# Agent attention and a maxout layer on one core: paired key tiles, 256-column output products, and the rare path's transfers on another queue

## The chip, the cores and the metric

The kernel runs on one core of one Trainium2 chip. The metric is the device time of one execution in microseconds (us). The kernel before took 259.56 us, the median of three runs (258.92 to 260.03).

## The reference

Four batches of 12,544 queries, keys and values of width 128, and 49 agents per batch. Agents attend over all keys, each query then attends over the 49 agents, and a layer with the maximum of three linear maps follows.

```python
def sm(a, b):
    s = scale * (a @ b.transpose(0, 2, 1))
    e = np.exp(s - s.max(-1, keepdims=True))
    return e / (e.sum(-1, keepdims=True) + 1e-09)
agent_v = sm(agents, k) @ v          # 49 x 128 per batch
x = sm(q, agents) @ agent_v          # 12544 x 128 per batch
h = np.maximum(np.maximum(x @ w1, x @ w2), x @ w3)   # 768 wide
out = h @ w_out
```

Everything comes in and goes out in float32: 77 MB of q, k and v in, 25.7 MB out.

## The kernel before, in words

All work is cut into tiles of 128 rows. A chunk of keys is 7 tiles (KT), a group of queries 8 tiles (GT); there are 14 chunks per batch and 49 groups in all (48 of one batch each, numbers 0 to 47, and number 48 of what is left of all four). SP issues every load and store of the ordinary path: three query groups, or up to four chunks of keys or values, in one transfer, into one of five buffers LD; results leave from five buffers OS, three groups at a time (line 521). A buffer is loaded again when its last reader is done.

Keys and values of batch b, per chunk: POOL casts K to bfloat16 (kc, line 300), PE turns the tiles (kt, 305), DVE takes them out of PSUM (ke, 311), PE makes the scores of 128 keys by 49 agents (ks), ACT the exponentials (kx, 320), ACT or POOL casts V (vc), and PE adds up the value products (kv, values, 322). This is done in eight products: one with a matrix of ones as the stationary operand and all 343 exponentials as the moving one, for the totals, and per tile one with V as the stationary and 49 exponentials as the moving operand. All of a batch's chunks are added up in one PSUM bank, acc. When a batch is through, normalise (nr, 368) reduces the seven totals, takes the reciprocal and scales.

From a batch's 49 by 128 result follow the small steps that make its matrix G (128 rows): the hidden units are sorted into those that are decided for all agents, whose part of the layer is linear, and at most 64 open ones, which the query groups compute. G holds U and V columns for the open units (GU, GV), a linear part (GL, written by linear_out, 494) and output rows for open units (GW). Rows 0 to 63 and 64 to 127 hold the same for the two halves of a pair of query tiles: in EQ, the exponentials of a group, rows 0 to 48 belong to one tile of a pair and rows 64 to 112 to the other.

Queries, per group s: POOL casts (qc), PE turns (qt), ACT takes out (qe, 541), PE makes scores (sc), ACT exponentials (ex, 554), PE sums (su) and DVE reciprocals (re); PE makes u and v, ACT a rectifier (a, 574), DVE the maximum into R (x, 577); out_products (p, 579) makes the output in two PSUM banks: for EQ with GL and for R with GW, for each of four pairs and each half, one product of half the rows and 128 columns, 16 in all. DVE scales both banks into OS (ov, out_scale, 595), and SP stores.

The order of all this is a list written out by hand (ORDER) with the buffer of each result behind the stroke; each engine takes its steps in that order, and waits by semaphores are put in from the buffers that a step reads and writes.

At the end DVE checks that all totals are in range (c0, c1, worst) and writes one number, most. All five engines load it and branch (lines 262 and 263): if it is over 64, a general path of the whole computation is run, of some 17,600 instructions, 520 of them SP's; otherwise they jump over it. With these inputs they jump. Behind the jump SP waits for all transfers, and the program ends.

## Time and profile before

| | before |
|---|---|
| median of three runs | 259.56 us |
| the profiled execution | 258.95 us |
| its span, first to last instruction | 257.1 us |
| mean granted TensorE clock | 0.911 |
| PE, DVE, ACT, POOL busy | 73%, 65%, 56%, 57% |
| moved by the DMA engines | 105.01 MB, 409 GB/s over the span |
| HBM read and written | 78.74 MB, 25.69 MB |

In the profile, PE is TensorE's matmuls and PEld its weight loads, which overlap; DVE is VectorE, ACT ScalarE, POOL GpSimd, SP SyncE with its queue of transfers (SPq). The queue q1 holds SP's loads and stores, q10 ScalarE's one transfer (the agents, line 214), q8 and q14 the blocks of instructions that the engines fetch as they go. A row of a group names line, engine, operation, what is written and read, the count, then busy us and mean ns of one, then idle time before it with what ended it. A row of the timeline begins with its start and its busy time in us. Matmuls are pipelined, so the busy time of a row is longer than the distance from its start to the next row's.

### The profile page before, as it was taken

Reading aid. Unit: us, or ns where it says so; the run is one execution under the profiler, and the core shown is the slowest. Engines: PE = TensorE matmul, PEld = TensorE weight load, DVE = VectorE, ACT = ScalarE, POOL = GpSimd, SP = SyncE. Lnnn points to the kernel's source line nnn. Section 1 sums busy time; section 2 is a strip of 40 time slices with the busy share of each in tenths; the row PEclk is TensorE's granted clock in tenths of the full one; section 3 lists DMA queues with packets and bytes.
Section 4 is the critical chain, followed back from the end, with each engine's and each line's share of the span. In section 5 each row is a group of like instructions: output and inputs, shape, how many; then the busy total and the mean of one; then the engine's idle time right before and its main releaser. Section 6 shows DMA issues by size and latency. Waiting matters only on the chain.

```text
span 257.1 us, 7504 instructions
## 1 busy us (share of the span) xinstructions
PE 187.8 (73%) x3071; PEld 138.0 (54%) x3106; DVE 166.3 (65%) x344; ACT 145.2 (56%) x240; POOL 145.6 (57%) x164
## 2 busy tenths in 40 slices
PE   0684675779798679895988699868688789997500
PEld 0462543658476458674775486446465466664200
DVE  4444422837677878864599955744729989888830
ACT  1445356328585656573666657646256868796400
POOL 2252652988789289786973997478464434440000
PEclk9998699779999979997699999999869999999855
DMA  7999999999999999999999999999999999999992
GB/s 257 435 415 416 427 420 426 420 426 419 420 418 425 423 422 427 424 418 423 418 426 424 419 425 425 426 416 421 424 432 421 421 410 431 423 423 426 410 370 85
DMA packets 11528, 105.01 MB, mean 409 GB/s; under 512 B 1176, under 2 KB 2396, under 8 KB 4444
## 3 DMA queue, kind: packets, MB, share of 16 engines
q1 hardware_dynamic: 11280, 104.34, 97.0%
q8 instruction: 26, 0.43, 0.7%
q10 hardware_dynamic: 203, 0.10, 0.1%
q14 instruction: 19, 0.15, 0.1%
HBM read 78.74 MB, written 25.69 MB: 406 GB/s over the span
## 4 chain that ended last, share of the span: by engine, by line
DMA 55%; POOL 12%; PE 12%; DVE 8%; ACT 5%; issue 3%; another core or an unknown queue 1%; SPq 0%; DVEq 0%; ACTq 0%; POOLq 0%
DMA LD<-in_v_dram 25%; DMA LD<-in_k_dram 14%; DMA out_dram<-OS 9%; PE psum L273 9%; POOL VB L300 6%; DMA LD<-in_moe_w_dram 5%; DVE OS L595 3%; POOL KB L300 3%; POOL QB L535 3%; PE psum L305 3%; DMA sums_of<-in_agents_dram 2%; ACT EQ L554 1%; ACT VB L298 1%; ACT QT L541 1%; DVE R L577 1%
## 5 line engine op out<-in xcount | busy, mean ns | idle before, releaser
L300 POOL CAST KB<-LD 128x896 bf16<-128x896 f32 x56 | 51.8, 964 | 36.2 <-DMA LD<-in_k_dram 35.2
L535 POOL CAST QB<-LD 128x1024 bf16<-128x1024 f32 x49 | 49.7, 1048 | 34.7 <-DMA LD<-in_q_dram 26.0
L595 DVE TENSOR_TENSOR OS<-psum,sums_of 128x512 f32<-128x512 f32 x97 | 60.7, 676 | 9.7 <-DMA out_dram<-OS 5.0
L541 ACT ACTIVATE QT<-psum 128x1024 bf16<-128x1024 bf16 x49 | 50.2, 1024 | 21.9 <-PE psum L305 20.2
L311 DVE COPY KT<-psum 128x896 bf16<-128x896 bf16 x56 | 34.5, 620 | 34.0 <-PE psum L305 29.8
L305 PE MATMUL psum<-ident,KB 128*128 128x128 bf16 x392 | 37.8, 249 | 11.3 <-POOL KB L300 10.2
L300 POOL CAST VB<-LD 128x896 bf16<-128x896 f32 x42 | 38.5, 956 | 5.8 <-DMA LD<-in_v_dram 5.4
L554 ACT ACTIVATE EQ<-psum 128x512 bf16<-128x512 f32 x49 | 29.3, 598 | 21.9 <-PE psum L273 15.9
L320 ACT ACTIVATE EK<-psum 128x343 bf16<-128x343 f32 x56 | 25.3, 459 | 25.4 <-PE psum L273 16.6
L305 PEld LDWEIGHTS <-KB 128*128 128x128 bf16 x392 | 29.2, 113 | 17.9 <-POOL KB L300 14.0
L305 PE MATMUL psum<-ident,QB 128*128 128x128 bf16 x392 | 31.9, 228 | 6.5 <-POOL QB L535 5.8
L574 ACT ACTIVATE AS<-psum 128x512 bf16<-128x512 f32 x49 | 29.1, 597 | 12.8 <-PE psum L273 12.3
L577 DVE TENSOR_TENSOR R<-psum,AS 128x512 bf16<-128x512 f32 x49 | 32.4, 676 | 5.8 <-ACT AS L574 2.2
L305 PEld LDWEIGHTS <-QB 128*128 128x128 bf16 x392 | 26.1, 102 | 15.2 <-POOL QB L535 8.4
L273 PEld LDWEIGHTS <-EQ 49*128 49x128 bf16 (+1 forms) x588 | 20.8, 97 | 16.9 <-ACT EQ L554 8.0
L273 PE MATMUL psum<-QT,agT 128*128 128x512 bf16 (+1 forms) x82 | 25.2, 374 | 6.2 <-ACT QT L541 5.7
L273 PE MATMUL psum<-EQ,G 128*128 128x512 bf16 (+1 forms) x91 | 28.0, 367 | 1.3 <-issue 0.6
L273 PEld LDWEIGHTS <-VB 128*128 128x128 bf16 x392 | 16.8, 97 | 17.7 <-ACT VB L298 8.9
L273 PE MATMUL psum<-EK,VB 128*128 128x49 bf16 x392 | 19.6, 187 | 6.4 <-ACT VB L298 5.2
L273 PE MATMUL psum<-agT,KT 128*128 128x49 bf16 x392 | 20.7, 192 | 1.5 <-DVE KT L311 0.9
L273 PE MATMUL psum<-G,EQ 49*128 49x128 bf16 x392 | 20.9, 223 | 1.2 <-DVE OS L595 0.5
L273 PE MATMUL psum<-G,R 64*128 64x128 bf16 x392 | 20.1, 223 | 1.4 <-DVE R L577 1.4
(89 smaller groups left out, 184.7 us busy)
## 6 DMA issues: line engine op xcount, KB each, us to landing
LD<-in_q_dram SPq DMA_DIRECT2D x16, 1536.0 KB, 17.7
out_dram<-OS SPq DMA_DIRECT2D x15, 1536.0 KB, 22.1
LD<-in_k_dram SPq DMA_DIRECT2D x12, 1792.0 KB, 16.3
LD<-in_v_dram SPq DMA_DIRECT2D x12, 1792.0 KB, 17.0
LD<-in_k_dram SPq DMA_DIRECT2D x4, 896.0 KB, 16.7
LD<-in_v_dram SPq DMA_DIRECT2D x4, 896.0 KB, 15.0
out_dram<-OS SPq DMA_DIRECT2D x3, 512.0 KB, 12.3
LD<-in_moe_w_dram SPq DMA_DIRECT2D x3, 384.0 KB, 13.6
```

Source lines behind the costliest of these rows:

```text
L273: self.nc.tensor.matmul(out, w, x, start=start, stop=True, skip_group_check=True)
L298: self.nc.scalar.activation(out, src, AF.Copy)
L300: self.nc.gpsimd.tensor_copy(out=out, in_=src)
L305: self.nc.tensor.transpose(t[:, j * P:(j + 1) * P], src[:, j, :], self.ident)
L311: return lambda: self.nc.vector.tensor_copy(out=self.t[f"kT{r}"], in_=self.t[f"kT_ps{r}"].bitcast(BF16)[:, :KT * C])
L320: return lambda: self.nc.scalar.activation(self.t[f"e{r}"], self.t[f"s{r}"][:, :KT * A], AF.Exp, scale=SCALE)
L535: return lambda: self.nc.gpsimd.tensor_copy(out=self.t[f"qb.{s}"], in_=self.half("q", s))
L541: return lambda: self.nc.scalar.activation(self.t[f"qT.{s}"].rearrange("p j c -> p (j c)"), self.t[f"qT_ps.{s}"].bitcast(BF16), AF.Copy)
L554: return lambda: self.nc.scalar.activation(self.t[f"e.{s}"], self.t[f"qs.{s}"], AF.Exp, scale=SCALE)
L574: return lambda: self.nc.scalar.activation(self.t[f"a.{s}"], self.t[f"u.{s}"], AF.Relu)
L577: return lambda: self.nc.vector.tensor_tensor(out=self.t[f"r.{s}"], in0=self.t[f"v.{s}"], in1=self.t[f"a.{s}"], op=ALU.max)
L595: self.nc.vector.tensor_tensor(out=out, in0=src, in1=rc.unsqueeze(2).to_broadcast([P, 4, C]), op=ALU.mult)
```

## The change

Value products (values): the exponentials of a tile now lie 64 apart (EK is 7 x 64 wide, cleared once at the start), and V's buffers have two more columns per tile, filled with ones once. Two tiles' exponentials, 128 columns, are the stationary operand and two tiles of V with their ones, 260 columns, the moving one; tile by tile the two blocks on the diagonal are what is wanted. A chunk is three such products and one of a single tile (64 by 130), and the totals come with the ones columns. At a batch's end DVE copies the two blocks into one tile (ne), PE turns and adds them with two float32 products against a folded identity (nt), and normalise (nr) takes the reciprocal and scales.

Output products (out_products): G's parts GL and GW are twice as wide and block-diagonal, the upper half of the rows with one tile's columns, the lower with the other's. One product takes all 128 rows and makes 256 columns, both tiles of a pair: 8 instead of 16 per group. The outputs of a bank are now four tiles in a row, and the scores read every second tile. Linear_out becomes two copies.

The products with rd and with pick are put one after the other, three small tiles share memory with cand, and the loads and stores of the general path are issued by ScalarE instead of SP.

PE at the output products of group 36, ahead of which stands u of group 39; EQ_90 holds group 36's exponentials, G_138 (before) and G_149 (after) are batch 3's G. Before:

```order
L273 LDWEIGHTS G_138
L273 MATMUL psum<-EQ_93,G_138 128x512
L273 LDWEIGHTS EQ_90
L273 MATMUL psum<-G_138,EQ_90 128x128
L273 LDWEIGHTS EQ_90
L273 MATMUL psum<-G_138,EQ_90 128x128
L273 LDWEIGHTS EQ_90
L273 MATMUL psum<-G_138,EQ_90 128x128
L273 LDWEIGHTS EQ_90
L273 MATMUL psum<-G_138,EQ_90 128x128
```

The same place after, up to the first product with R:

```order
L285 LDWEIGHTS G_149
L285 MATMUL psum<-EQ_93,G_149 128x512
L285 LDWEIGHTS EQ_90
L285 MATMUL psum<-G_149,EQ_90 128x256
L285 LDWEIGHTS EQ_90
L285 MATMUL psum<-G_149,EQ_90 128x256
L285 LDWEIGHTS EQ_90
L285 MATMUL psum<-G_149,EQ_90 128x256
L285 LDWEIGHTS EQ_90
L285 MATMUL psum<-G_149,EQ_90 128x256
L285 LDWEIGHTS R_101
L285 MATMUL psum<-G_149,R_101 128x256
```

Nothing is moved past another step; eight products of 128 columns have become four of 256, for EQ and again for R.

PE in one chunk of keys, between the scores of one chunk and of the next; EK_96 holds exponentials, VB_78 the cast V. Before, the first rows of eight products:

```order
L273 MATMUL psum<-agT,KT_81 128x49
L273 LDWEIGHTS ones
L273 MATMUL psum<-EK_96,ones 128x343
L273 LDWEIGHTS VB_78
L273 MATMUL psum<-EK_96,VB_78 128x49
L273 LDWEIGHTS VB_78
L273 MATMUL psum<-EK_96,VB_78 128x49
```

After, all of them:

```order
L285 MATMUL psum<-agT,KT_81 128x49
L285 LDWEIGHTS EK_96
L285 MATMUL psum<-VB_78,EK_96 128x260
L285 LDWEIGHTS EK_96
L285 MATMUL psum<-VB_78,EK_96 128x260
L285 LDWEIGHTS EK_96
L285 MATMUL psum<-VB_78,EK_96 128x260
L285 LDWEIGHTS EK_96
L285 MATMUL psum<-VB_78,EK_96 64x130
L285 LDWEIGHTS KT_82
```

The product with ones, which read only exponentials, is gone, and the first product of a chunk now reads the cast V.

SP after its last stores; LD_65 is a load buffer. Before, the general path's loads follow the branch:

```order
L521 DMA out_dram<-OS_105 128x1024 x2
L521 DMA out_dram<-OS_105 128x512 x2
L262 TENSOR_LOAD most
L263 COMPARE_AND_BRANCH
L618 DMA LD_65<-in_k_dram 128x896 x15
L634 DMA LD_66<-in_v_dram 128x896
```

After, to the end of SP's program:

```order
L550 DMA out_dram<-OS_105 128x1024 x2
L550 DMA out_dram<-OS_105 128x512 x2
L274 TENSOR_LOAD most
L275 COMPARE_AND_BRANCH
L275 UNCONDITIONAL_BRANCH x2
```

SP's 520 instructions of the general path are one now, and ScalarE has 516 more in it (1428 instead of 912). In the ordinary part PE has 1224 instructions fewer, counting those that only wait (4990 instead of 6214).

The diff, cut to its core (ORDER has `ne` and `nt` put ahead of each `nr`, and nothing else):

```diff
-GU, GV, GL, GW, GC = 0, P, 2 * P, 3 * P, 4 * P
+GU, GV, GL, GW, GC = 0, P, 2 * P, 4 * P, 6 * P
+VC = C + 2
...
-            add(f"kv{r}", PE, em.values(b, g), mm(2 * KT, 49), after=[f"kx{r}", f"vc{r}"] + ([f"kv{b}.{g - 1}"] if g else []),
+            add(f"kv{r}", PE, em.values(b, g), mm(KT // 2, 2 * VC), after=[f"kx{r}", f"vc{r}"] + ([f"kv{b}.{g - 1}"] if g else []),
...
-        add(f"nr{b}", DVE, em.normalise(b), (0.62, 0.75), after=[f"kv{b}.{NCH - 1}"], use=[f"acc{b}"])
+        add(f"ne{b}", DVE, em.key_evacuate(b), (0.35, 0.5), after=[f"kv{b}.{NCH - 1}"], use=[f"acc{b}"])
+        add(f"nt{b}", PE, em.key_turn(b), (0.6, 0.85), after=[f"ne{b}"], use=[f"acc{b}"])
+        add(f"nr{b}", DVE, em.normalise(b), (0.25, 0.4), after=[f"nt{b}"], use=[f"acc{b}"])
...
+        self.fold = const.tile([P, A], FP32, name="fold")
+        for h in range(2):
+            nc.vector.tensor_copy(out=self.fold[h * H:(h + 1) * H, :], in_=self.ident[h * H:(h + 1) * H, h * H:h * H + A])
+        for e in self.slots["EK"]:
+            nc.vector.memset(e, 0.0)
+        for v in self.slots["VB"]:
+            nc.vector.memset(v[:, :, C:], 1.0)
...
     def values(self, b, g):
         def fn():
             acc, e, vb = self.t[f"acc{b}"], self.t[f"e{b}.{g}"], self.t[f"vb{b}.{g}"]
-            self.mul(acc[:, :KT * A], self.ones, e, g == 0)
-            for j in range(KT):
-                self.mul(acc[:, KT * H:KT * H + A], vb[:, j, :], e[:, j * A:(j + 1) * A], False)
+            for j in range(0, KT, 2):
+                n = min(2, KT - j)
+                self.mul(acc[:n * H, :n * VC], e[:, j * H:(j + n) * H], vb[:, j:j + n, :].rearrange("p j c -> p (j c)"), g == 0 and j == 0)
...
+    def key_evacuate(self, b):
+        def fn():
+            for h in range(2):
+                r = slice(h * H, (h + 1) * H)
+                self.nc.vector.tensor_copy(out=self.av[r, :], in_=self.t[f"acc{b}"][r, h * VC:(h + 1) * VC])
+    def key_turn(self, b):
+        def fn():
+            t = self.t[f"acc{b}"][:, 2 * VC:]
+            self.mul(t[:, :A], self.av[:, :C], self.fold, True)
+            self.mul(t[:, H:H + A], self.av[:, C:C + 1].to_broadcast([P, P]), self.fold, False)
...
-            self.nc.vector.tensor_reduce(out=kr, in_=acc[:, :KT * A].rearrange("p (j a) -> p a j", a=A), op=ALU.add, axis=AX)
-            self.nc.vector.reciprocal(kr, kr)
-            self.nc.vector.tensor_tensor(out=self.avT[b][:, :A], in0=acc[:, KT * H:KT * H + A], in1=kr, op=ALU.mult)
+            self.nc.vector.reciprocal(kr, t[:, H:H + A])
+            self.nc.vector.tensor_tensor(out=self.avT[b][:, :A], in0=t[:, :A], in1=kr, op=ALU.mult)
...
-            for src, c, k in (("e", GL, A), ("r", GW, H)):
+            for src, c in (("e", GL), ("r", GW)):
                 for jj in range(GT // 2):
-                    for h in range(2):
-                        r = slice(h * H, h * H + k)
-                        self.mul(self.t[f"o.{s}.{h}"][:, jj * C:(jj + 1) * C], self.t[f"{src}.{s}"][r, jj * P:(jj + 1) * P],
-                                 self.G[of[jj]][r, c:c + C], src == "e" and jj == 0)
+                    self.mul(self.t[f"o.{s}.{jj // 2}"][:, jj % 2 * 2 * C:(jj % 2 + 1) * 2 * C], self.t[f"{src}.{s}"][:, jj * P:(jj + 1) * P],
+                             self.G[of[jj]][:, c:c + 2 * C], src == "e" and jj % 2 == 0)
...
-            nc.sync.dma_start(kf[:, :KT, :], rows("k", b, g))
+            nc.scalar.dma_start(kf[:, :KT, :], rows("k", b, g))
...
-                nc.sync.dma_start(vf[:, :KT, :], rows("v", b, g))
+                nc.scalar.dma_start(vf[:, :KT, :], rows("v", b, g))
```

More of the change, by code (lines that the diff above doesn't have):

```diff
@@ L177, in graph @@
         add(f"x.{s}", DVE, em.max_second(s), dve(512), after=[f"v.{s}", f"a.{s}"], new=[("R", f"r.{s}")], use=[f"v.{s}", f"a.{s}"])
-        add(f"p.{s}", PE, em.out_products(s), (0.5, 0.72), after=[f"x.{s}", f"ex.{s}"] + gy, new=[("M", f"o.{s}.{h}") for h in range(2)],
+        add(f"p.{s}", PE, em.out_products(s), (0.9, 1.1), after=[f"x.{s}", f"ex.{s}"] + gy, new=[("M", f"o.{s}.{h}") for h in range(2)],
             use=[f"e.{s}", f"r.{s}"])
@@ L519, in fn @@
             if h is not None:
[L520 removed]
+                far, near = (x[:, 4 * h:4 * h + 4, :] for x in (far, near))
             self.nc.sync.dma_start(far, near)
         return fn
[L524 to L526 removed]
     def rc(self, s):
```

71 lines of the change are left out of this document (40 added, 31 removed).

## The prediction

> **What bounds the kernel now.** I read the page's slices and queues first, then busy time by stretch, then the end.
>
> ```profile
> PE 187.8 (73%) x3071; PEld 138.0 (54%) x3106; DVE 166.3 (65%) x344; ACT 145.2 (56%) x240; POOL 145.6 (57%) x164
> ...
> DMA  7999999999999999999999999999999999999992
> GB/s 257 435 415 416 427 420 426 420 426 419 420 418 425 423 422 427 424 418 423 418 426 424 419 425 425 426 416 421 424 432 421 421 410 431 423 423 426 410 370 85
> ...
> q1 hardware_dynamic: 11280, 104.34, 97.0%
> q8 instruction: 26, 0.43, 0.7%
> q14 instruction: 19, 0.15, 0.1%
> ...
> LD<-in_q_dram SPq DMA_DIRECT2D x16, 1536.0 KB, 17.7
> out_dram<-OS SPq DMA_DIRECT2D x15, 1536.0 KB, 22.1
> ```
>
> The DMA engines are full from the second slice to the last but two, at about 420 GB/s, and 97.0% of their time belongs to q1, the loads and stores. A transfer of 1.57 MB needs 3.7 us at that rate, yet lands 17.7 to 22.1 us after its issue: some 14 us of others stand ahead of it. The bytes do not change, so an engine that is late by less than that changes nothing until the last stores. The end has to be read by itself; here are the stretches from 199 us, when no load is left to issue, with busy us of PE, PEld, DVE, ACT, POOL, the clock, the DMA share and GB/s.
>
> ```profile
> 199.00:208.00 9.00, 6.66 (x84) 4.00 (x81) 8.47 (x21) 6.93 (x12) 4.10 (x5) 1.00 1.01 419
> 208.00:216.00 8.00, 7.80 (x148) 5.50 (x147) 7.21 (x16) 6.82 (x13) 4.00 (x4) 1.00 1.02 418
> 216.00:224.00 8.00, 7.53 (x129) 5.25 (x132) 6.92 (x16) 6.70 (x11) 3.01 (x3) 1.00 1.01 428
> 224.00:232.00 8.00, 7.38 (x119) 4.90 (x116) 6.75 (x14) 6.84 (x11) 3.01 (x3) 1.00 1.00 423
> 232.00:240.00 8.00, 6.57 (x101) 4.11 (x102) 7.02 (x16) 4.82 (x8) 0.00 (x0) 1.00 1.00 420
> ...
> 247.00:257.10 10.10, 0.00 (x0) 0.00 (x0) 0.00 (x0) 0.00 (x0) 0.00 (x0) 0.50 0.44 172
> ```
>
> Here PE and DVE are nearly full while the DMA still never idles; compute is finished at 247, and the DMA engines empty for ten microseconds more. The next lines are the chain's last piece; SP's queue of its last stores and its waits at the branch (line 263), from 240 us on; the DMA share of the last 27 us in 40 slices of 0.68 us, with the code blocks of that time and the landing of the last pair of stores.
>
> ```profile
> 246.67 0.16 DVE most L458
> ```
> ```profile
> 240.33 4.15 SPq L521 DMA_DIRECT2D out_dram<-OS  x4
> ```
> ```profile
> SPq L263 <- SPq L263: 7.7, 2, 6.8
> ```
> ```profile
> DMA  9999999999999999999999999877767531200000
> ...
> q8 instruction: 3, 0.05, 0.7%
> q14 instruction: 9, 0.07, 0.7%
> ...
> out_dram<-OS SPq DMA_DIRECT2D x2, 256.0 KB, 11.3
> ```
>
> The last store is issued at about 244 and lands 11.3 us later, at 255.3; the span ends 1.8 us after that. The verdict is known at 246.83; SP then waits at the branch twice, 7.7 us in all, which brings it from about 247.5 to that landing. From slice 26 (247 us) the share falls: some DMA engines are done, others go on to slice 35 (254 us). So the slowest DMA engine sets the end, and two paths run beside each other in the last ten microseconds: stores to land, and all engines taking the branch over the general path, for which code is fetched (9 of the 19 blocks of q14 fall in these 27 us).
>
> **Part 1, output products (out_products).** One group before is eight G,EQ and eight G,R products; rows of PE, start and busy us:
>
> ```profile
> 102.39 0.40 PE L273 MATMUL psum<-G,EQ 49*128 49x128 bf16 x8
> 102.63 0.39 PE L273 MATMUL psum<-G,R 64*128 64x128 bf16 x8
> 102.85 0.39 PE L273 MATMUL psum<-G,EQ 49*128 49x128 bf16 x8
> 103.08 0.39 PE L273 MATMUL psum<-G,R 64*128 64x128 bf16 x8
> 103.40 0.62 PE L305 MATMUL psum<-ident,QB 128*128 128x128 bf16 x8
> ```
>
> Two groups take 103.40 - 102.39 = 1.01 us, 0.50 each: 0.23 per eight, 29 ns per product of 128 columns, and 0.09 lost where it goes over to full-height products. The last row's products have 128 columns as well, at full height, and last 0.62 for eight, so the half-height ones overlap in pairs. After, eight full-height products of 256 columns. Their pace from 512 columns:
>
> ```profile
> 97.58 0.38 PE L273 MATMUL psum<-EQ,G 128*128 128x512 bf16 x1
> 97.80 0.38 PE L273 MATMUL psum<-QT,agT 128*128 128x512 bf16 x1
> ```
>
> 0.22 per 512, so 0.11 per 256 and 0.88 per group: +0.38 us, or +0.3 if the way into the half-height products costs as much as the way out. The Trainium skill, TensorEngine Tiling (Array Packing), Theoretical Speedup and Key Properties, gives up to twice the speed for at most 64 rows and a drain at each change of mode, which speaks against giving the tiles up: by it the group would grow by 0.46 and win the drains back, +0.37 for the one seen. The trace agrees, by 29 ns against 55 per 128 columns and by the 0.09. How many groups stand where:
>
> ```profile
> 0.00:199.40 199.40, 13.25 (x256) 9.17 (x256) 22.09 (x33) 0.92 1.00 417
> ```
>
> That is PE's time on the tile R: 256 products, 32 groups, before 199.4, so 17 of 49 after. The 32 cost 12 us of PE spread over 199, behind the queue of 14 us: nothing. For the last 17, PE gains 6.5 us of work. From 208 to 232 it has 24 - 22.71 = 1.3 us idle, and the 11 groups there add 4.2: 2.9 us late. From 232 to 240 it has 1.4 us idle against five groups' 1.9, but DVE sets the pace there. So the last store is issued D = 3 us later, at 247; bounds 0 (DVE hides it, since a first bank is complete two products earlier) and 6.5.
>
> **Does D move the end?** Not by the stores: the slowest DMA engine has work until about 254 and its share of the last stores comes before that as long as D is under some 8 us; the quick ones idle meanwhile. By the branch it may: 246.83 + D = 250 is left with 7 us to the end instead of 10.3. If those 10.3 are rigid, all 3 us show. If code is fetched at leisure beside the stores, none does. SP's two waits end with the landing, so SP had slack; of the other four engines no row tells. I take 0 for the likeliest, since after 250 the fetches meet engines at a share of 0.3 to 0.5 instead of 0.7.
>
> **Part 2, value products (values), k_exps, casts.** Rows of two groups before:
>
> ```profile
> 101.64 0.32 PE L273 MATMUL psum<-EK,ones 128*128 128x343 bf16 x1
> 101.79 0.34 PE L273 MATMUL psum<-EK,VB 128*128 128x49 bf16 x7
> 101.98 0.31 PE L273 MATMUL psum<-EK,ones 128*128 128x343 bf16 x1
> ```
>
> 0.34 per group; after, three of 260 columns and one of 130 at the pace above, 0.39. So 56 x 0.05 = 2.8 us more of PE, all before 199: 0. Added wait: the product with ones needed only the exponentials, now the first product waits for the cast of V too; behind it on PE stand transposes and scores of the next chunks, and POOL waits for their buffers. 0.15 us at a time, under the queue. If that cover were gone, it would be 56 x 0.2 = 11 us.
>
> **Part 3, totals.** Rows of what goes and of the nearest to what comes:
>
> ```profile
> L371 DVE TENSOR_REDUCE sums_of<-psum 128x49 f32<-128x343 f32 x4 | 2.0, 510 | 5.2 <-PE psum L273 5.2
> ...
> L494 DVE CAST G<-psum 128x256 bf16<-128x256 f32 x4 | 1.7, 425 | 4.2 <-PE psum L273 4.1
> ...
> L226 DVE MEMSET G<- 128x256 uint32 x4 | 1.1, 272 | 0.0
> ...
> L277 DVE CAST ag_bf<-sums_of 49x512 bf16<-49x512 f32 x1 | 0.9, 947 | 2.6 <-DMA sums_of<-in_agents_dram 2.6
> ...
> L284 DVE COPY slot_of<-psum 128x64 f32<-128x64 f32 x1 | 0.2, 217 | 0.0
> ```
>
> The reduction of 0.51 goes; two copies of 0.25 to 0.3 and two float32 products come, which the trace does not show: 0.2 us each as any small one, to 0.9 at four passes. Chain per batch: +0.4 to +1.9 us, four times. PE's new wait for the copies has behind it the next batch's first transposes in batch 0, for which DVE waits, and query products in the others, 0.6 us at a time. The order puts a batch's first query groups several microseconds behind it, and for batches 0 to 2 the DMA queue hides it. Batch 3 lies near 200 us: up to 1 us there, taken into D's bounds. Linear_out in two copies, +0.2 us on DVE per batch, likewise. The prologue gains four clears of EK (224 words, 0.24), G half as long again (4 x 0.14), four short fills and two casts: about 1.9 us on DVE, which idles 2.6 before ag_bf: 0. Tiles that now share cand's memory are used one after another as before, and the scores read as many columns of QT, every second tile: 0.
>
> **Part 4, fewer instructions.** PE loses 392 + 224 products with their weight loads and gains 8 pairs: 1216 instructions of 2 x 3106. The 26 q8 blocks are 0.43 MB / 26 = 16 KB each; taken as PE's stream, 239 instructions to a block, 5 go. One costs 0.7% x 16 x 257.1 / 26 = 1.1 us of one DMA engine; five are 5.5 us, spread over 16 engines 0.34. Bounds: 0 (blocks on engines that finish early) and -1.1 (one fewer on the slowest). I take -0.3. The Trainium skill, Runtime: NRT & Kernel Launch, Instruction fetch mechanics, gives blocks of 256 instructions and calls their cost mostly hidden, which would make this term 0; the 16 KB agree with it, the full DMA engines speak against hidden.
>
> **Part 5, the general path's transfers on ScalarE's queue.** They do not run. SP's code behind the branch becomes short, so perhaps two blocks of q14 fewer in the last 8 us: 0.7% x 16 x 27 / 9 = 0.34 us each on one engine. Between 0 and -0.7, and only if it is the slowest; 0. ACT, off the path there, jumps further.
>
> **Sum.** The profiled execution took 258.95: span 257.1 and 1.85 around it. -0.3 makes 258.65. The median of the runs shown is 0.61 higher, so 259.3.
>
> **Rivals.** A: DMA still sets the end, 259.3; its own range is 258.5 (blocks at -1.1 instead of -0.3) to 260.1 (no gain, 259.6, and the 0.5 us by which the runs shown lie above their median). For it: the full share to 247 and the emptying after; 0.70.
> B, slower: the verdict path. PE is late by D at 199 to 240 us, the branch follows, and code fetch ends after the last landing. It decides once D exceeds the slack of that path. With D = 3 and no slack 259.3 + 3 = 262.3; with half of it 260.8. For it: 7.80 of 8 busy on PE, 9 blocks fetched in the tail. Against: SP's waits. 0.20. The same page's section says that a taken branch outside the fetched window stalls for a fetch; that is this mechanism, and the late q14 blocks agree.
> C, faster: the slowest DMA engine loses a whole PE block and both of SP's: -1.1 - 0.7, so 257.8. For it: the taper from 247.7 to 254, in which single blocks weigh fully. Against: which engine serves them is not shown. 0.10. That the change does nothing to the time at all lies in A.
>
> A measurement of this kernel tells 0.5%, 1.3 us, from no change. C lies below 258.3, B's larger half above 260.9; the range 258.1 to 261.6 holds A whole, half of B and part of C. Faster 0.10, same 0.72, slower 0.18.
>
> **What would show it.** Right: bytes and share unchanged to 247 us; a group of output products at 0.85 to 0.9 us; 21 blocks on q8; the last store issued near 247 and landed by 255.3; span 256 to 258. B: the most row near 250 and SP's wait at the branch short, with idle DMA engines before the end. Wrong: the DMA share under 9 tenths before 240 us, PE above 95% there, or an end that moves by over 2 us with the last landing.

## The result and the profile after

| | before | after |
|---|---|---|
| median | 259.03 us (258.73 to 260.03, 18 runs) | 255.18 us (254.59 to 258.82, 18 runs) |
| after / before | | 0.9852, 95% interval 0.9838 to 0.9866 |
| the profiled execution | 258.95 us | 256.11 us |
| its span | 257.1 us | 254.3 us |
| mean granted TensorE clock | 0.911 | 0.948 |

The kernel became faster by 1.5%, 3.85 us; the forecast was no change, 259.3, with a range from 258.1. About 0.5 us of that distance is its base: it stood on a median of 259.56 us over three runs, and over 18 the kernel before takes 259.03. Below, a difference of two kernels in us is the difference of their ratios to the kernel before, times 259.0. Two of the runs of the kernel after, at 258.5 and 258.8 us, were disturbed and are left out of the ratio. The profiled execution of the kernel after, 256.11 us, lies 0.9 us above its median, so its span shows 2.8 of the 3.85 us.

The page of the kernel after: busy time, DMA share and GB/s in 40 slices of the span, and the queues.

```profile
PE 207.8 (82%) x2484; PEld 152.4 (60%) x2506; DVE 169.9 (67%) x362; ACT 146.2 (57%) x240; POOL 145.1 (57%) x164
...
DMA  6999999999999999999999999999999999999992
GB/s 251 439 430 418 432 426 426 432 422 435 422 418 426 428 430 427 428 427 422 431 424 434 423 432 426 428 426 424 426 425 429 425 421 430 422 427 425 399 401 80
...
q1 hardware_dynamic: 11280, 104.34, 97.2%
q8 instruction: 20, 0.33, 0.5%
...
q14 instruction: 16, 0.13, 0.1%
```

The queue q1 has the same 11280 packets and 104.34 MB as before, and the DMA engines are as full as before from the second slice on. But what they move in that time is more: most slices read 422 to 435 where most read 415 to 427. Busy time by stretch says it in one row. First the kernel before from 10 to 236 us (the last two numbers are the DMA share and GB/s), then the kernel after, with stretches that answer to those of the prediction:

```profile
10.00:236.00 226.00, 180.81 (x2983) 133.44 (x3017) 151.62 (x298) 138.59 (x229) 142.52 (x154) 0.93 1.01 422
```
```profile
10.00:236.00 226.00, 198.61 (x2408) 146.00 (x2428) 152.34 (x303) 138.35 (x228) 142.00 (x154) 0.95 1.01 427
...
208.00:216.00 8.00, 7.92 (x121) 6.27 (x122) 7.14 (x16) 6.16 (x12) 3.42 (x4) 1.00 1.01 428
...
232.00:240.00 8.00, 7.08 (x72) 5.08 (x71) 6.70 (x15) 6.23 (x9) 0.00 (x0) 1.00 0.98 407
...
247.00:254.30 7.30, 0.16 (x1) 0.00 (x0) 1.06 (x6) 0.00 (x0) 0.00 (x0) 0.59 0.29 112
```

At an equal share, 104.34 MB take 247.3 us at 422 GB/s and 244.4 us at 427: 2.9 us less, about what the span lost. Behind 247 us some 0.8 MB are left to move (112 GB/s over 7.3 us) instead of 1.7 (172 GB/s over 10.1 us), so the stores are done sooner. The transfers also land sooner (KB each, median us from issue to landing), the last pair of stores within 5.7 us:

```profile
LD<-in_q_dram SPq DMA_DIRECT2D x16, 1536.0 KB, 15.6
out_dram<-OS SPq DMA_DIRECT2D x15, 1536.0 KB, 18.3
...
out_dram<-OS SPq DMA_DIRECT2D x2, 256.0 KB, 5.7
```

TensorE's rows answer to the costs of the products; each begins with start and busy us:

```profile
64.95 0.67 PE L285 MATMUL psum<-VB,EK 128*128 128x260 bf16 x4
65.56 0.61 PE L285 MATMUL psum<-QT,agT 128*128 128x512 bf16 x2
...
239.90 0.60 PE L285 MATMUL psum<-G,EQ 128*128 128x256 bf16 x4
...
240.34 0.60 PE L285 MATMUL psum<-G,R 128*128 128x256 bf16 x4
...
240.77 0.24 PE L285 MATMUL psum<-sel,EQ 128*128 128x2 bf16 x4
...
242.15 3.97 SPq L550 DMA_DIRECT2D out_dram<-OS  x4
...
248.29 0.16 DVE L485 SCALAR_TENSOR_TENSOR most<-good,gap 128x1 int32<-128x1 f32 x1
```

A group of output products takes 240.77 - 239.90 = 0.87 us, as worked out; a chunk of value products takes 0.61 us, not 0.39. The verdict, and with it the last store's issue, comes 1.6 us later than before (248.29 against 246.67). SP's waits from 236 us on show that the end has changed hands (engine and line, waited for, us in total, times, longest):

```profile
SPq L275 <- SPq L275: 2.5, 2, 1.8
SPq L274 <- DVE most L485: 2.3, 1, 2.3
...
SPq L860 <- PEq L275: 1.0, 1, 1.0
```

At the branch SP waits 2.5 us instead of 7.7, and then, with all stores landed, 1.0 us for TensorE, which is still on its way over the general path (it branched at 249.1 and goes on at 253.3).

### The profile page after: what moved, and what is told of

Read it like the earlier page. It is cut to its first block, busy times and chain, and to the rows that moved or that the text cites. A ratio compares the mean times of both kernels' runs of the same rounds, so it can differ in the third digit from the quotient of the medians.

```text
span 254.3 us, 6336 instructions
## 1 busy us (share of the span) xinstructions
PE 207.8 (82%) x2484; PEld 152.4 (60%) x2506; DVE 169.9 (67%) x362; ACT 146.2 (57%) x240; POOL 145.1 (57%) x164
## 3 DMA queue, kind: packets, MB, share of 16 engines
q1 hardware_dynamic: 11280, 104.34, 97.2%
## 4 chain that ended last, share of the span: by engine, by line
PE 63%; DVE 12%; ACT 9%; DMA 7%; issue 4%; POOL 2%; ACTq 0%; DVEq 0%; POOLq 0%
PE psum L285 48%; PE psum L317 15%; DMA LD<-in_k_dram 5%; ACT QT L566 4%; DVE OS L618 3%; DMA sums_of<-in_agents_dram 2%; ACT EQ L579 2%; ACT VB L310 1%; DVE gap L435 1%; POOL KB L312 1%; ACT AS L599 1%; DVE KT L323 1%; DVE R L602 1%; DVE cand L434 1%; ACT EK L334 1%
## 5 line engine op out<-in xcount | busy, mean ns | idle before, releaser
L285 PE MATMUL psum<-VB,EK 128*128 128x260 bf16 x224 | 39.7, 279 | 4.9 <-ACT VB L310 3.0
L317 PE MATMUL psum<-ident,KB 128*128 128x128 bf16 x392 | 34.7, 238 | 4.2 <-POOL KB L312 3.4
L285 PEld LDWEIGHTS <-EK 128*128 128x128 bf16 x224 | 21.0, 102 | 24.4 <-issue 16.4
L285 PE MATMUL psum<-QT,agT 128*128 128x512 bf16 (+1 forms) x104 | 29.6, 371 | 6.1 <-ACT QT L566 5.9
L285 PEld LDWEIGHTS <-EQ 128*128 128x128 bf16 x392 | 25.7, 97 | 11.9 <-ACT EQ L579 6.9
L317 PEld LDWEIGHTS <-KB 128*128 128x128 bf16 x392 | 27.6, 107 | 8.5 <-POOL KB L312 4.0
L317 PE MATMUL psum<-ident,QB 128*128 128x128 bf16 x392 | 30.3, 221 | 0.1
L285 PE MATMUL psum<-G,R 128*128 128x256 bf16 x196 | 29.4, 273 | 1.2 <-DVE R L602 1.2
L285 PE MATMUL psum<-G,EQ 128*128 128x256 bf16 x196 | 29.4, 272 | 0.2
L285 PE MATMUL psum<-EQ,G 128*128 128x512 bf16 (+1 forms) x82 | 24.5, 363 | 1.0 <-DVE sums_of L589 0.4
```

What stands on the lines that cost most here:

```text
L285: self.nc.tensor.matmul(out, w, x, start=start, stop=True, skip_group_check=True)
L317: self.nc.tensor.transpose(t[:, j * P:(j + 1) * P], src[:, j, :], self.ident)
```

## Experiments: the pace of the DMA engines

Which part of the change could make the same packets faster? One candidate is a side effect. Three small tiles now share memory with cand, G is wider, fold is new, and so the buffers that are laid out behind them moved:

```diff
-        self.w1_bf = const.tile([P, DFF], BF16, name="w1_bf")
-        self.w1T = const.tile([P, NF, P], BF16, name="w1T")
...
+        flat = self.cand.rearrange("p i f a -> p (i f a)")
+        self.w1_bf = flat[:, :DFF // 2].bitcast(BF16)
+        self.w1T = flat[:, DFF // 2:DFF].bitcast(BF16).rearrange("p (f c) -> p f c", c=P)
```

Per partition, w1_bf and w1T took 3072 bytes of their own; the four G take 2048 more and fold, with its padding, 224, so what lies behind comes 800 bytes earlier. In the compiled kernel before, the first load buffer LD starts at byte 42528 of each partition, 32 behind a multiple of 256; in the kernel after it starts at 41728, a multiple of 256. The five buffers are 14336 bytes each, 56 times 256, so all five start alike. The store buffers OS start 32 behind a multiple of 256 before and 128 behind one after. Theory P is that this place sets the pace. The rival, theory W, is that the saved work does it: fewer instructions, fewer blocks of code to fetch.

**b_ld224** and **b_ld32**: the kernel before with an unused tile ahead of everything (56 columns, or 8).

```diff
+        const.tile([P, 56], FP32, name="pad")
         self.ident = const.tile([P, P], BF16, name="ident")
```

> The kernel before, with an unused tile of 224 bytes put ahead of all others, so that each of its buffers starts 224 bytes later in a partition: the load buffers LD at a multiple of 256 (as in the kernel after) instead of 32 behind one, the store buffers OS at a multiple of 256 instead of 32 behind one. No instruction is added, removed or moved. Theory P (place): where the load buffers start sets what a packet of the DMA engines costs; the 14 KB packets, which lasted mostly 539 ns before and 535 ns after, then last 535, GB/s rise from about 420 to about 427, and the time falls by what the packets save, 2.9 us of 259.0: 256.1, at 255.3 to 257.0. Theory W (work): the gain came from fewer instructions and fewer blocks of code to fetch, or from TensorE's other products; then this kernel takes 259.0 as before, within 0.5, and GB/s stay at 420.

Measured: 256.82 us, ratio 0.9916 (0.9900 to 0.9933), 2.2 us faster without one instruction changed. The stretch of b_ld224 has the GB/s of the kernel after:

```profile
10.00:236.00 226.00, 184.80 (x3007) 137.05 (x3040) 154.14 (x303) 140.80 (x233) 142.15 (x154) 0.91 1.01 427
```

> The kernel before, with 32 unused bytes ahead of all buffers: LD and OS start 64 bytes behind a multiple of 256. No instruction changes. By theory P it tells how fine the place must be: if a multiple of 64 is enough, 256.1 (255.3 to 257.0), as with LD at a multiple of 256; if it takes 128 or 256, 259.0 within 0.6. Theory W: 259.0 within 0.5 either way.

Measured: 258.89 us, 0.9993 (0.9979 to 1.0006). A start 64 behind a multiple of 256 gains nothing that the time shows.

**a_ld32** and **a_ld128**: the same tile with 8 and with 32 columns in the kernel after.

> The kernel after, with an unused tile of 32 bytes put ahead of all others: LD starts 32 bytes behind a multiple of 256, as in the kernel before, OS 160 behind one. No instruction changes. Theory P: the packets go back to about 539 ns, GB/s to 420, and the time to 255.2 + 2.9 = 258.1, at 257.5 to 259.4; what is left between it and 259.0 is what the change's work gives by itself. Theory W: 255.2 within 0.5, GB/s 427.

Measured: 257.06 us, 0.9933 (0.9917 to 0.9950): 2.1 us of the gain are gone, less than the 2.9 that were expected, and 1.7 us against the kernel before stay. So P holds for about 2 us, and something else gives the rest.

> The kernel after with an unused tile of 128 bytes ahead of all others: LD at 128 behind a multiple of 256 (64 behind did not help the kernel before), OS at a multiple of 512. No instruction changes. If the load buffers must start at a multiple of 256: packets of 14 KB over 535 ns, time up to 257.1. If 128 is enough: 255.2 within 0.4.

Measured: 255.87 us, 0.9870 (0.9849 to 0.9891), 0.5 us slower than the kernel after, with overlapping intervals. Packets say more than the time does (table below): 128 is nearer to 64 than to 256.

**a_os32** and **a_ldonly**: which buffers? An unused buffer of 32 bytes ahead of the store buffers OS; or one of 32 ahead of LD and one of 224 behind it.

```diff
-SLOTS = {"M": 8, "LD": 5, "QB": 3, "KB": 3, "VB": 4, "KT": 3, "QT": 3, "EQ": 8, "EK": 4, "AS": 3, "R": 3, "OS": 5}
+SLOTS = {"M": 8, "LD": 5, "QB": 3, "KB": 3, "VB": 4, "KT": 3, "QT": 3, "EQ": 8, "EK": 4, "AS": 3, "R": 3, "PAD": 1, "OS": 5}
```

```diff
-SLOTS = {"M": 8, "LD": 5, "QB": 3, "KB": 3, "VB": 4, "KT": 3, "QT": 3, "EQ": 8, "EK": 4, "AS": 3, "R": 3, "OS": 5}
+SLOTS = {"M": 8, "PAD": 1, "LD": 5, "PAD2": 1, "QB": 3, "KB": 3, "VB": 4, "KT": 3, "QT": 3, "EQ": 8, "EK": 4, "AS": 3, "R": 3, "OS": 5}
```

> The kernel after, with 32 unused bytes ahead of the store buffers alone: LD stays at a multiple of 256, OS starts 160 bytes behind one and no longer at a multiple of 64. No instruction changes. Theory P with loads alone: 255.2 within 0.5, since the stores' packets were 460 ns at the end of both traces. Theory P with stores too: they are a quarter of the bytes, so a quarter of 2.9 us comes back, 255.9 (255.6 to 256.5). Theory W: 255.2 within 0.5.

Measured: 255.12 us, 0.9853 (0.9837 to 0.9870): moving OS from 128 to 160 behind a multiple of 256 costs nothing. It does not compare with a start at a multiple; for that there are the stores' packets, below.

> The kernel after with 32 unused bytes ahead of the load buffers LD and 224 behind them: LD alone starts 32 bytes behind a multiple of 256, all other buffers keep their place to the byte of 256. No instruction changes. Theory P, loads: the price is that of all buffers shifted, 257.06 against 255.18, so 257.1 (256.6 to 257.6), with 14 KB packets of 539 to 546 ns. If it is the place of a buffer that engines read or write instead (QB, KB, VB, KT, OS): 255.2 within 0.4.

Measured: 256.81 us, 0.9909 (0.9893 to 0.9926): 1.5 us slower than the kernel after, at 423 GB/s, with no buffer but LD moved against the multiples of 256. This and the 2.1 us of a_ld32 lie within each other's intervals. The stretch:

```profile
10.00:236.00 226.00, 200.78 (x2417) 146.20 (x2417) 151.50 (x302) 137.71 (x227) 142.03 (x154) 0.95 1.01 423
```

The packet records of the traces give the cause its size. A packet of 14336 bytes is a partition's piece of a load of keys or values; those of 12288 are queries and stores, half of each.

| LD's start behind a multiple of 256 | kernel | 14336 B, median and mean | 12288 B, share at 460 ns |
|---|---|---|---|
| 32 | before | 539, 542.5 ns | 0.63 |
| 32 | a_ldonly | 539, 542.7 ns | 0.62 |
| 64 | b_ld32 | 538, 541.4 ns | 0.68 |
| 128 | a_ld128 | 538, 540.6 ns | 0.77 |
| 0 | b_ld224 | 535, 536.9 ns | 0.96 |
| 0 | after | 535, 537.1 ns | 0.96 |
| 0 | a_os32 | 535, 537.1 ns | 0.95 |

The stores' own packets can be told apart from 230 us on, when the last load has landed (by 226.7 us before): those of 12288 bytes last 463.3 ns on average with OS at 32 behind a multiple of 256 (before), 463.1 at a multiple (b_ld224), 463.3 at 128 (after) and 463.6 at 160 (a_os32). So for stores no price of the place is seen.

All packet times of an execution, shared by 16 engines, are 252.12 us before, 250.11 in b_ld224 and 249.22 after. One per cent of a packet is little, but until the last ten microseconds these engines do not idle, and so it is nearly one per cent of the time: 2.0 us of packets, 2.2 us measured. The Trainium skill, DMA: Bandwidth & Descriptors, How a descriptor splits into AXI transactions, says that transactions start at multiples of 256 bytes, and that a piece that starts elsewhere begins with bytes that are fetched and not used. It says so of what a transaction reads. The traces agree on the 256, but for the side that is written: a load's target in the buffers LD; for the stores, which read the buffers OS, no price was seen.

## Experiments: the other 1.7 us

**b_act**: of the kernel before, only the general path's four transfers.

```diff
-            nc.sync.dma_start(kf[:, :KT, :], rows("k", b, g))
+            nc.scalar.dma_start(kf[:, :KT, :], rows("k", b, g))
...
-            nc.sync.dma_start(self.far("out", s, GT), self.near(s, out, GT))
+            nc.scalar.dma_start(self.far("out", s, GT), self.near(s, out, GT))
```

> The kernel before with nothing changed but the general path's loads and stores, issued by ScalarE instead of SP (the last part of the change, alone). LD stays 32 behind a multiple of 256. If SP's short program saves fetched blocks at the end (q14 from 19 to about 16) and these lie on the slowest DMA engine: 258.9 - 0.3 to - 0.9, so 258.0 to 258.6; if they lie beside the stores: 258.9 within 0.3. Slower if ScalarE's longer way over the path sets the end: 259.2 or more.

Measured: 257.78 us, 0.9938 (0.9919 to 0.9957), 1.6 us faster than before, more than the larger of the gains that were expected (0.9). These transfers never run. From 244 us on, blocks of code before and in b_act:

```profile
q14 instruction: 8, 0.07, 1.2%
q8 instruction: 2, 0.03, 1.0%
```
```profile
q14 instruction: 6, 0.05, 1.0%
q8 instruction: 2, 0.03, 0.9%
```

**b_ld224_act**: b_ld224 and b_act together.

> The kernel before with two things: LD at a multiple of 256 (224 unused bytes ahead of all buffers) and the general path's transfers on ScalarE. Neither changes an instruction of the ordinary path. If the two are independent: 259.0 - 2.1 - 1.3 = 255.6 (255.2 to 256.0), so that next to nothing of the 3.85 us is left for the value and output products. If the products do carry a part: 256.5 or more.

Measured: 255.66 us, 0.9869 (0.9843 to 0.9895). The two add up, and 0.4 us are left to the kernel after, within the intervals: next to nothing for the products from which the change has its name.

**a_sp**: the kernel after with the four transfers back on SP.

> The kernel after with the general path's loads and stores back on SP; nothing else is undone, and all buffers keep their places. In the kernel before, this part alone gave 1.2 to 1.6 us (257.78). Theory J (jump): SP, which waits for the last landing, needs code from beyond the path, and the blocks for it, one of them behind the landing, are what it cost; then 255.2 + 1.2 = 256.4. If the end of the kernel after is set by TensorE's way over the branch instead (SP waited 1.0 us for TensorE there), up to 1.0 of that is hidden: 255.4 to 256.4. If the 1.2 came from another cause than SP's program: 255.2 within 0.3.

Measured: 255.96 us, 0.9886 (0.9860 to 0.9911), 0.9 us slower than the kernel after. SP's wait there:

```profile
SPq L275 <- SPq L275: 3.8, 1, 3.8
```

The verdict was written by 247.95, and the last store landed at 251.57; SP branched at about 248.6 and went on only 3.8 us later, at 252.38, when its other waits followed within 0.1 us each. All stores had landed by then, so it was its code that it waited for. With the transfers on SP its own jump thus ends 0.8 us behind the last landing. In the profiled executions this does not show in the end, since both spans are 254.3 us, a_sp's by SP and the kernel after's by TensorE; the 0.9 us are those of the medians. The Trainium skill, Runtime: NRT & Kernel Launch, Instruction fetch mechanics, says that a taken branch to code outside of the fetched window stalls until the code is there; this wait agrees.

**b_nobr, b_ld224_nobr, a_nobr**: no branch and no general path, so nothing to jump over and nothing to fetch at the end. These kernels leave out the rare case; all ordinary work stays.

```diff
-        worst = self.nc.values_load(self.most[:1, :1], skip_runtime_bounds_check_because=why)
-        with self.tc.If(worst > CAPACITY):
-            self.in_general()
```

> The kernel before without the branch at its end and without the general path: the verdict is computed and not read, no engine loads it, jumps or fetches code from beyond a path, and SP only waits for the landings. LD stays 32 bytes behind a multiple of 256. Theory J: the way over the branch costs the kernel before in its last 8 us, by blocks fetched on DMA engines that still have stores and by SP's code, and ScalarE's taking the transfers removed part of that (1.2 us); without any branch at least that much goes: 257.0 to 257.8. If that 1.2 us had another cause: 258.6 to 259.0.

Measured: 256.54 us, 0.9893 (0.9877 to 0.9910), 2.8 us less than with it.

> The kernel before with LD at a multiple of 256 and without the branch and the general path. Against the kernel after without the branch it has the old products and 5 blocks of code more, but no other difference that ends late. If the products' worth is their code: 0.3 to 0.8 us more than the kernel after without the branch. If they are worth nothing: the same within 0.3.

Measured: 253.96 us, 0.9793 (0.9777 to 0.9810).

> The kernel after without the branch and the general path, as told of the kernel before. If in the kernel after the engines' way over the branch sets the end (SP waited 1.0 us for TensorE behind the last landing): what is left is the landing at 251.2 + 0.4 and 1.75 us of ending, less what the fetched blocks held up, 253.3 or less, so 254.2 to 255.0 instead of 255.18. If the landing sets it and the branch lies beside it: 255.2 within 0.3.

Measured: 253.88 us, 0.9789 (0.9772 to 0.9805). The page of a_nobr has 19 and 10 blocks of code, none of them from 244 us on, and SP waits for the last stores alone:

```profile
q8 instruction: 19, 0.31, 0.4%
...
q14 instruction: 10, 0.08, 0.1%
```
```profile
SPq L857 <- DMA out_dram<-OS: 7.4, 1, 7.4
```

A branch that jumps over what never runs costs 2.8 us in the kernel before, 3.2 in b_ld224 and 1.6 in the kernel after. And without it b_ld224 and after take the same time: 0.1 us apart, interval 0.6 to either side. The products' own worth is nothing that this can tell. The two differ by 5 blocks of code on q8 as well (24 and 19), so those are not seen to cost anything either. Where the branch's price lies is read from the records of the profiled executions, one of each kernel: when the last packet of a store ended, when the last store was reported as landed, which is what SP waits for, and when the span ended.

| | last packet | last landing | end | landing to end |
|---|---|---|---|---|
| before | 254.47 | 255.25 | 257.07 | 1.82 |
| b_act | 253.69 | 254.13 | 255.95 | 1.82 |
| b_nobr | 253.34 | 253.76 | 254.82 | 1.06 |
| b_ld224 | 252.62 | 253.50 | 255.32 | 1.82 |
| b_ld224_act | 251.83 | 252.25 | 254.07 | 1.82 |
| b_ld224_nobr | 250.69 | 251.12 | 252.18 | 1.06 |
| a_sp | 251.22 | 251.57 | 254.27 | 2.70 |
| after | 251.14 | 251.49 | 254.31 | 2.82 |
| a_nobr | 250.96 | 251.30 | 252.37 | 1.06 |

In the kernel before SP's two waits at the branch end at 254.29 and 255.27, each 0.02 us behind a landing of its stores (254.28 and 255.25). Its code was there by then, so the landing set the end, as the prediction had read it. The branch makes that landing 1.5 us later (255.25 against 253.76) and what follows it 0.8 us longer. The move to ScalarE brings the landing forward by 1.1 us in b_act and by 1.25 in b_ld224_act, and changes nothing behind it. In the kernel after it is the other way round: 0.2 us of the branch's price lie ahead of the landing and 1.8 behind it, where SP waits for TensorE. That is shown in size, by one execution of each kernel. That the part ahead of the landing comes from blocks of code on DMA engines that still have stores is argued from the counts (8, 6 and 0 blocks of q14 before, in b_act and in b_nobr); which engine serves which block stands in no record.

**b_late**: the kernel before, verdict 3 us later.

```diff
+        for _ in range(16):
+            nc.vector.tensor_scalar(out=self.good[:, :1], in0=t[:, :1], scalar1=-8.0, scalar2=8.0 * P, op0=ALU.mult, op1=ALU.add)
```

> The kernel before with the first operation of the verdict repeated 16 times on VectorE, so that the number that all engines branch on comes about 3 us later, at about 249.8; the stores are not touched. It tests step D of the prediction, that 3 us less between verdict and end cost nothing. If the fetch of code runs at leisure beside the stores: 259.0 within 0.4. If the way over the branch is rigid: 262. In the trace of before TensorE is over the branch at 1.6 us ahead of the last landing and SP asks for it 2.5 us later, so between them: 259.0 to 259.6.

Measured: 259.36 us, 1.0014 (1.0004 to 1.0024): 0.4 us for 3 us. The way over the branch is shorter when it starts later: TensorE took 6.0 us for it before (247.6 to 253.6) and 3.9 here (250.6 to 254.5). The last store, too, lands 1.0 us earlier, at 254.29, with the same eight blocks of q14 fetched later, which agrees with the argument above. Now SP's code comes last, at 255.39: its wait at the branch shrinks from 7.7 to 4.8 us, in one piece, as in a_sp:

```profile
SPq L263 <- SPq L263: 4.8, 1, 4.8
```

**a_split, a_split_nobr**: every output and value product in two, with and without the branch, for the price of TensorE's code.

```diff
                 for jj in range(GT // 2):
-                    self.mul(self.t[f"o.{s}.{jj // 2}"][:, jj % 2 * 2 * C:(jj % 2 + 1) * 2 * C], self.t[f"{src}.{s}"][:, jj * P:(jj + 1) * P],
-                             self.G[of[jj]][:, c:c + 2 * C], src == "e" and jj % 2 == 0)
+                    for i in range(2):
+                        self.mul(self.t[f"o.{s}.{jj // 2}"][:, (jj % 2 * 2 + i) * C:(jj % 2 * 2 + i + 1) * C], self.t[f"{src}.{s}"][:, jj * P:(jj + 1) * P],
+                                 self.G[of[jj]][:, c + i * C:c + (i + 1) * C], src == "e" and jj % 2 == 0 and i == 0)
...
-                self.mul(acc[:n * H, :n * VC], e[:, j * H:(j + n) * H], vb[:, j:j + n, :].rearrange("p j c -> p (j c)"), g == 0 and j == 0)
+                for i in range(n):
+                    self.mul(acc[:n * H, i * VC:(i + 1) * VC], e[:, j * H:(j + n) * H], vb[:, j + i, :], g == 0 and j == 0 and i == 0)
```

> The kernel after with every product of out_products and of values cut in two by columns, 128 + 128 and 130 + 130, each half with a weight load of its own: 1120 instructions more on TensorE (560 products and 560 weight loads), the same columns, rows and bytes of data, the same places of all buffers. Of the 1.8 us that the change is worth at an equal place of LD (256.82 against 255.18 us with LD at a multiple of 256; 258.94 against 257.06 with LD 32 behind one), theory F (fetch) says that they are the 5 blocks of code that the DMA engines no longer fetch for TensorE: then about 4 of these come back (q8 from 21 to 25), and the time is 255.2 + 0.8 * 1.8 = 256.6, at 256.1 to 257.2. Theory T (tail): they come from the later, denser end of compute, not from the number of instructions: 255.2 within 0.5, with 25 blocks as well.

Measured: 256.84 us, 0.9914 (0.9877 to 0.9951), too wide to be of much use, and its verdict came 1.1 us later than in the kernel after (249.38), which confounds it.

> The kernel a_split (every output and value product cut in two, 1120 instructions more on TensorE, 5 blocks of code more) without the branch and the general path. Without the branch the later verdict can cost nothing, so that what it takes more than the kernel after without the branch is what the 5 blocks cost at the DMA engines. Theory F: 0.3 (what the blocks last, shared by 16 engines) to 0.8 us (with the stalls of packets beside them, and the slowest engine). If code is fetched at no cost: 0 within 0.3; then what a_split cost was the later verdict.

Measured: 254.52 us, 0.9817 (0.9801 to 0.9834), 0.7 us more than a_nobr, interval 0.6 to either side. But here too the verdict, and with it the work ahead of it, is later, by 2.8 us (248.84 against 246.04). So 0.7 us is what 1120 instructions in 5 blocks and the later work cost together. Theory F is not refuted, only bounded.

**a_oldp**: the kernel after with the old output products.

```diff
-            for src, c in (("e", GL), ("r", GW)):
+            for src, c, k in (("e", GL, A), ("r", GW, H)):
...
+                    for h in range(2):
+                        r = slice(h * H, h * H + k)
```

> The kernel after with the output products of before: G's parts of 128 columns, 16 products of half the rows per group, the scores' and stores' old choice of tiles, linear_out in one copy; the new value products, the placement of all buffers and the general path on ScalarE stay. It has 784 instructions more on TensorE than after. Theory F: 3 blocks more, so 0.6 of 1.8 us come back: 256.3. Theory V (verdict): in the kernel after the last store lands 3 us before the end, and the branch with its fetches, which starts with the verdict at 248.45, sets the end; the old products give the verdict 1.6 us earlier, so 253.6 at best, and the stores' landing plus its 1.9 us of ending would be next, near 253.5 to 255. Both at once: 254.5 to 256.

Measured: 255.07 us, 0.9833 (0.9809 to 0.9857), not told from the kernel after, below the 256.3 of theory F alone and within what it and an earlier verdict together were expected to give.

**a_c0, a_oldp_c0**: most of the totals' check 17 us earlier, in the kernel after and in a_oldp.

```diff
-qt.44/3 ov.41.1 ex.43/4
+qt.44/3 ov.41.1 c0 ex.43/4
...
-st.47.0 st.47.1 c0 c1 good worst
+st.47.0 st.47.1 c1 good worst
```

> The kernel after with the large part of the totals' check (c0, three operations of 1.85 us on VectorE over 532 totals that are all known by then) moved in the list from behind the last stores to behind ov.41.1, some 17 us earlier. Nothing is added or left out. If the verdict and the way over the branch set the end after (1.3 us over the kernel without a branch, 255.18 against 253.88), the verdict comes up to 1.9 us earlier and most of that goes: 254.2 to 254.9. If VectorE, nearly full there, only pushes the stores back by what it saves at the end: 255.2 within 0.4.

Measured: 255.42 us, 0.9864 (0.9833 to 0.9895): no gain, the second of the two cases. The verdict came 0.9 us earlier only, since VectorE's work ahead of it was pushed back, and TensorE was still last over the path, by 0.7 us:

```profile
SPq L860 <- PEq L275: 0.7, 1, 0.7
...
SPq L274 <- DVE most L485: 0.4, 1, 0.4
```

> The same move of c0 in the kernel a_oldp (new value products, old output products, LD at a multiple of 256, the general path's transfers on ScalarE), whose last stores and verdict are earlier than in the kernel after. It measured 255.07. Expected: its end is set by the landings beside the branch, so less is to be had than in a_c0: 254.4 to 255.1. If it stays at 255.1 while a_c0 falls, the output products' cost was in the verdict alone.

Measured: 254.96 us, 0.9836 (0.9814 to 0.9857). Nothing tried with the general path in it is faster than the kernel after by more than the intervals.

## Why the prediction was wrong

**The step that failed first** is in the reading of what bounds the kernel: "The bytes do not change, so an engine that is late by less than that changes nothing until the last stores." That the DMA engines bound the kernel was right, and so was the sentence as far as it goes, but the forecast took from it that their pace does not change either. Bytes are not time. The pace rose by 1%, because the change resized tiles that lie ahead of the load buffers; b_ld224 and a_ldonly show it with no instruction changed. That is about 2.1 of the 3.85 us (1.5 to 2.6 by the pair that is compared), and no term of the sum had a place for it. The prediction named the resized tiles ("Tiles that now share cand's memory are used one after another as before"), costed them at 0 as work, and did not ask what lies behind them.

**Part 5, the general path's transfers,** was mis-sized: "Between 0 and -0.7, and only if it is the slowest; 0." Measured: -1.6 alone, -1.2 on top of the better place, 0.9 back when undone. The count of two blocks was right (8 to 6 from 244 us on), and so was the place: in b_act and b_ld224_act it is the last landing that comes earlier, by 1.1 and 1.25 us, and nothing else. Their worth there is what it had too small: at most 0.7 us at 0.34 us a block, and 0 was chosen. Why the landing moves by more than the blocks last stays open. The prediction had no price for the whole way over the path either, which is 2.8 us before.

**Part 1, the output products:** the size was right, 0.87 us for a group against 0.88 worked out. D was forecast at 3 us; the verdict is 1.6 us later, but that is net of the faster loads. With LD at one place it is 1.3 and 2.3 us later (a_ld32 and a_ldonly against before), 4.6 (after, b_ld224) and 2.5 (a_nobr, b_ld224_nobr), so 3 was about right. That D moves the end by next to nothing was right within 0.4 us (b_late), where the way over the branch became shorter by starting later, as had been argued. In the kernel after, however, the branch has become what ends last, with 1.0 us of SP waiting for TensorE.

**Part 2, the value products,** had a wrong price: 0.61 us for a chunk instead of 0.39, so 56 x 0.27 = 15 us more of TensorE instead of 2.8. TensorE's busy time rose by 20 us, 187.8 to 207.8. The pace of the 260-column products was right, 0.11 us each; what was left out lies around the fourth product, of 64 by 130: 0.09 us more ahead of it and 0.12 behind it. The queue hid it all the same, as the term said.

**Part 4, fewer blocks of code:** 20 blocks on q8, forecast 21. Its -0.3 with bounds 0 and -1.1 is not contradicted: five blocks show 0.1 us, interval 0.6 to either side (a_nobr, b_ld224_nobr), and at most 0.7 with later work (a_split_nobr). Part 3 left no trace.

**The rivals.** A, at 0.70, fails by the pace. B had the right mechanism and the wrong price: the way over the branch does end last in the kernel after, but a verdict 3 us later costs 0.4 us, not 1.5 to 3. C, at 0.10, took 1.8 us off its base of 259.56 for fewer blocks on the slowest engine; with the load buffers at the old place the change takes 1.7 us off (a_ld32). So C was nearest to what the written change does, but that its sum fits is in part luck: its SP part of 0.7 measured 0.9 to 1.6, and its PE block of 1.1 was not seen. The other half of the gain no case had. Of the signs of being wrong, two came: TensorE is busy for 7.92 of the 8 us from 208 to 216, which cost nothing, and the end moved with the last landing, by 3.8 us in the profiled executions.

## What to carry to other kernels

Where the DMA engines are always full, their pace is a term of the sum like any other: ask of every change of a tile's size where it puts the buffers that transfers write to, and let them start at a multiple of 256 bytes on purpose. Code that never ran was paid for at the jump over it, and taking most of it away from the engine that waits for the last landing gave 0.9 to 1.6 us here. And when a change has several parts, an unused tile that puts the buffers back is a cheap control.

## What the runs showed of the hardware that was not expected

- A load whose target starts 32 bytes behind a multiple of 256 had packets of 542.5 ns on average, at a multiple 537.1; 64 and 128 behind gave 541.4 and 540.6. Over the kernel this was 1.5 (a_ldonly) to 2.6 us (b_nobr against b_ld224_nobr) of 259. For the source of stores, at 0, 32, 128 and 160 behind, no such difference was seen.
- The value products, three of 260 columns and one of 130, took 0.6 us for 910 columns, while four of 256 took 0.44 us for 1024. The trace of the kernel after puts the difference at the product of 64 by 130: the products start at 0, 0.11, 0.23 and 0.43 us, and what follows them at 0.60, with the granted clock at 1.00. In a_split, with six products of 130 columns ahead of it 0.06 us apart, it starts 0.15 us behind the last of them, and what follows 0.18 us behind it. Why is open; no run here varied that product's shape.
- A branch over a path that is not run cost 1.6 to 3.2 us at the end of the program, by what stands next to it.
